# A local attention and gated feed-forward kernel on one core: orders for VectorE and GpSimd as one resource, values over 128 partitions, first mixing by TensorE, normalisation and mixing on any of three engines

## The chip, the cores and the metric

The kernel runs on one core of one Trainium2 chip. A core has TensorE (PE in the profile, with PEld for its weight loads), VectorE (DVE), ScalarE (ACT), GpSimd (POOL) and SyncE (SP), which issues all loads and stores here. The metric is device time in microseconds (us); less is better.

## The reference

Four batches, eight heads, 768 tokens, head size 64. First a local attention with pooled blocks, then a feed-forward layer with a sigmoid gate on its output:

```python
k_sum = k.reshape(B, H, nb, block, D).max(axis=3)        # block = 32, nb = 24
v_sum = v.reshape(B, H, nb, block, D).mean(axis=3)
mask_l = np.abs(pos[:, None] - pos[None, :]) < window    # window = 16
scores_l_m = np.where(mask_l, scale * q @ k.T, -1e9)
scores_s = scale * einsum(q, k_sum) + np.log(block)
a = softmax(concatenate([scores_l_m, scores_s]))
x = a @ concatenate([v, v_sum])                          # -> (4, 768, 512)

x_prev = x shifted by one token
xk = mu_k * x + (1.0 - mu_k) * x_prev
xr = mu_r * x + (1.0 - mu_r) * x_prev
k = np.maximum(xk @ w_k, 0.0)                            # 512 -> 1024
v = k * k @ w_v                                          # 1024 -> 512
r = 1.0 / (1.0 + np.exp(-(xr @ w_r)))                    # 512 -> 512
return r * v
```

The weights arrive as 64-bit numbers and are made into 32-bit ones on the chip.

## The kernel before, in words

The work falls into operations that a planner (class `Plan`, method `schedule`) puts into an order for each engine before anything is emitted; the engines then run these orders strictly. The planner is a list scheduler: every operation has a length per engine from the table `LENGTH`, a due time, and the buffers that it takes from small pools; at each step the operation that can start first goes next, and among those that are ready, the one due first. `NUDGE` shifts due times by hand, by tag: `e` for a first product, `f` for a second one (with batch, half and index), `gate`, `mix`, `set`, `unit`, and the weights `wk`, `wv`, `wr`. Where an operation has a second way (`other`), an engine takes it only if no other engine would end it earlier by the planner's reckoning. The planner's numbers decide only on the order; the times on the chip are its own.

The stages:

- **Weights** (`weight`, lines 326 to 361). Twenty pieces of 512 KB (4 of w_r, 8 of w_k, 8 of w_v), three staging buffers `st`. Each is loaded, scaled (line 323 on ScalarE or 326 on GpSimd), its sign is taken on GpSimd (line 331), two VectorE steps join the bits (lines 335, 339), a cast makes the high part (347 or 349), and a VectorE subtraction makes the low part (361). All products are made of three in a fast format: high by high, high by low, low by high.
- **Sets** (`load_set`): for each batch and pair of heads, keys and two halves of the values are loaded (line 382: tiles of 120 partitions, one for each of 120 keys of a window, by 6 windows of 128), keys are pooled on VectorE (392 to 404), values by TensorE in batch 0 (416, 436) and spread (444).
- **Units** (`unit`): for each pair and half of the tokens, scores on TensorE (480), mask and minimum on VectorE (491), exponential on ScalarE (495), the reciprocal of the sum (502), six normalisations of 128 x 120 on GpSimd (506), transposes on TensorE (513), a copy (517), the products with the values (535), and their copy to `vx` (547 or 549).
- **Mixing** (`mixes`, lines 560 to 571): a scaled copy on ScalarE or GpSimd, a multiply-add on VectorE, a cast on ScalarE to the high part, a VectorE subtraction for the low part. It is done for the gate and for the first products, for each half and pair. `mixes_pe` does the two first steps by TensorE; no half uses it before the change.
- **Gate** (612 to 628) and **experts** (644 to 702): for each half, three gates with a sigmoid; eight first products (644), relu, square, high and low part (649 to 655), and eight second products (666, the last 692), then the product with the gate and the store.

Batch 0 needs the weights, its units and its mixing at the same time. From batch 1 on, a batch's units run in between the products of the batch ahead of it. Until the first gate, up to 150 spare matmuls on the identity (line 727) keep TensorE at work where it would wait.

Of the kernel before, what the change touches and what calls it, by code (L numbers as in the profile page):

```python
# [20 lines left out]
P = 128  # L21
# [18 lines left out]
    score=900, transpose=340, vtrans=200, vpool=900, vsel=240, spread=560, spread_p=900, values=1000, values0=1750, mixe=1480, minus=200, diag=330, none=0, wminus=1250, wevac=570, gate=2790, gate_p=2100, gate32=3720, e1=2090, e1_32=2800,  # L40
    e2a=1400, e2b=700, e2=700, e2h=350, resulth=400, e2_32=2800, e2l_32=930,
    warm=220, kred=860, kred2=470, kmax=190, kcopy=340, vred=860, mask=204, rc=190, evac=475, mixd=620, sub=490, khv=340,
    result=695, wsign=720, eps=190, wor=740, wsub=625, tiny=60,
    exp=380, pts=400, vm=160, mixa=540, cast=440, relu=525, square=530, sigmoid=500, wscale=570, wcast=530,
    norm=470, wscale_p=640, wcast_p=640, mixa_p=860, kcopy_p=630, evac_a=375, fill=735,
# [9 lines left out]
WARM = 150  # L55
APART = False
MIX_PE = ()
# [4 lines left out]
    e003=-1000, e004=8000, e005=3000, e013=-40000, e016=-20000, e017=-3000, f000=-8000,  # L62
    f001=3000, f002=3000, f003=-1000, f005=1000, f006=25000, f007=9000, f010=25000,
    f011=8000, f013=3000, f014=-20000, f015=3000, f017=25000, gate01=-3000, gate10=-8000,
    mix010=-8000, set12=7000, set13=3000, unit001=-3000, unit020=1000, unit100=1000, unit101=16000,
    unit110=8000, unit111=-9000, unit120=-39000, unit130=8000, unit131=11000, wk1=3000, wk3=20000,
    wk4=3000, wk6=4000, wk7=-20000, wr0=-21000, wr3=8000, wv3=7000, wv4=3000,
    wv5=-1000, wv6=-8000, wv7=-19000,
# [7 lines left out]
BETWEEN = 5, 6, 7  # L76

# [14 lines left out]
class Plan:  # L92
# [9 lines left out]
    def op(self, eng, cost, due, emit, reads=(), writes=(), size=0, other=None):  # L102

        bufs = []
        for x, _ in list(reads) + list(writes):
            if isinstance(x, Buf) and x not in bufs:
                bufs.append(x)
        ways = {eng: (LENGTH.get(cost, 0), emit)}
        if other:
            ways[other[0]] = (LENGTH[other[1]], other[2])  # L110
        o = Op(len(self.ops), ways, due, bufs, size)
        o.tag = self.tag
        for x in reads:
# [12 lines left out]
        self.ops.append(o)
        o.name = cost
        return o

    def schedule(self):  # L130
# [20 lines left out]
        order = []  # L151

# [8 lines left out]
        spare = [o for o in self.ops if o.name == "warm"]  # L161
        while any(ready.values()):
            best = None
            for e, now in engines.items():
                pick = None
                for o, at in ready[e]:
                    start, need, ok = max(at, now, o.due - EARLY if e == "SP" else 0), {}, True
                    for x in o.bufs:
                        if x.t is None:
                            k = need.get(x.pool, 0)  # L170
                            if x.n != turn[x.pool] + k or len(free_slots[x.pool]) <= k:
                                ok = False
                                break
# [29 lines left out]
            if e == "SP":  # L203
                engines[e] = start + 60
                dma = max(dma, start + 600) + o.size * DMA_NS_PER_BYTE
                o.finish = dma + DMA_FIXED - 600
            else:
                engines[e] = start + o.cost
                o.finish = start + o.cost + TAIL[e]
            for x in o.bufs:  # L210
# [6 lines left out]
            if o.name == "gate_p" and spare:  # L217

                for w in spare:
                    for x in w.bufs:  # L220
                        x.left -= 1
                        if not x.left:
                            free_slots[x.pool].append((start, x.t))
                spare = []
                ready["PE"] = [x for x in ready["PE"] if x[0].name != "warm"]
            if o.name == "warm":
                spare.remove(o)
# [8 lines left out]
def tile_kernel(ctx: ExitStack, tc: tile.TileContext, q, k, vT, v, mask, ident, pool, sel, mu, w_k, w_v, w_r, out):  # L236
# [50 lines left out]
    for which in kinds:  # L287
        for p in range(NPAIR):
            for n, m in enumerate((om_sb, mu_sb)):
                op("POOL", "diag", None, lambda which=which, p=p, n=n, m=m: nc.gpsimd.tensor_scalar(  # L290
                    out=diag_sb[:, kinds.index(which), p, n, :], in0=ident_sb, scalar1=m[:, which, p:p + 1], scalar2=1.0,
                    op0=ALU.mult, op1=ALU.mult), reads=[*IDENT, *OM, *MU], writes=[("diag", (which, p, n))])
            op("POOL", "none", None, lambda: None, reads=[("diag", (which, p, n)) for n in range(2)], writes=[("diag", (which, p))])
# [12 lines left out]
    def weight(name, i, src, dst_h, dst_l, due=None):  # L306
# [23 lines left out]
        def sign():  # L330
            nc.gpsimd.tensor_scalar(  # L331
# [12 lines left out]
        op("POOL", "wsign", None, sign, reads=[(st, 0)], writes=[(we, 0)])  # L344
# [26 lines left out]
    def load_set(b, p):  # L371
# [9 lines left out]
        for hf in range(2):  # L381
            op("SP", "load", None, lambda hf=hf: nc.sync.dma_start(
                out=windows(vw[hf]), in_=v[b, p, hf]),
               writes=[(vw[hf], "a"), (vw[hf], "b")], size=NK * HW * 512)
# [73 lines left out]
    def unit(b, p, hf, e, due):  # L458
# [45 lines left out]
        for h in range(2):  # L504
            for i in range(NSL):
                op("POOL", "norm", None, lambda h=h, i=i: nc.gpsimd.tensor_scalar(  # L506
                    out=y[h].t[:, i, :], in0=y[h].t[:, i, :], scalar1=rc.t[:, NSL * h + i:NSL * h + i + 1],
                    scalar2=1.0, op0=ALU.mult, op1=ALU.mult),
                   reads=[(y[h], i), (rc, 0)], writes=[(y[h], i)])
# [42 lines left out]
    def mixes(b, hf, which):  # L552
# [3 lines left out]
        for p in range(NPAIR):  # L556
# [6 lines left out]
               other=("POOL", "mixa_p", lambda xt=xt, xa=xa, p=p: nc.gpsimd.tensor_scalar(  # L563
                   out=xa.t, in0=xt.t[:, lo:lo + HT], scalar1=om_sb[:, which, p:p + 1], scalar2=1.0,
                   op0=ALU.mult, op1=ALU.mult)))
# [11 lines left out]
    def mixes_pe(b, hf, which):  # L577
# [4 lines left out]
        for p in range(NPAIR):  # L582
# [3 lines left out]
            def mix(xt=xt, ps=ps, p=p):  # L586
                for n in range(2):
                    nc.tensor.matmul(
                        ps.t[:, 0:HT], diag_sb[:, kinds.index(which), p, n, :], xt.t[:, n + lo:n + lo + HT], start=(n == 0), stop=False)

            op("PE", "mixe", None, mix, reads=[*old, (xt, hf), ("diag", (which, p))], writes=[(ps, 0)])
# [133 lines left out]
    spare = pools["av"][0][:, HT:HT + P]  # L725
    for _ in range(WARM):
        op("PE", "warm", 1.0e8, lambda: nc.tensor.matmul(spare, ident_sb, ident_sb, start=True, stop=True), reads=IDENT)  # L727
# [122 lines left out]
```

## Time and profile before

| what | value |
|---|---|
| median of 3 runs | 472.68 us (472.26 to 473.19) |
| profiled execution, span | 472.4 us |
| mean granted TensorE clock | 0.989 |
| instructions | 9665 |
| moved by DMA | 51.18 MB |

The page gives no other time of the profiled execution than its span, from the first instruction to the last; the median of the runs stands 0.3 us above it. "Busy" is the time in which an engine works on an instruction, and an instruction that waits inside the engine, for memory for instance, counts as busy. A group row shows line, engine, operation, what it writes and reads, the shapes and the count, then busy time and the mean of one, then the engine's idle time before it and what ended that. The chain of waits follows the last instruction back to what released it. In the windows, each engine has its busy us and its number of instructions; then come the granted clock, the DMA share and GB/s.

### The profile page before, as it was taken

The numbers are of one execution on the slowest core, as the hardware profiler recorded it, in microseconds if no ns is written. First come the engines' busy times: TensorE is split into PE (matmuls) and PEld (weight loads), VectorE is DVE, ScalarE is ACT, GpSimd is POOL, SyncE is SP. The second block draws the span as 40 slices with busy tenths as digits, with TensorE's granted clock in tenths as the row PEclk, the third lists the DMA queues.
The fourth block names the chain that finished last, engine by engine and source line by source line (L and its number), as shares of the span: only waits on it lengthen the run. The fifth ranks groups of instructions, "written<-read, shape, count | busy, mean of one in ns | idle before, by whom it ended". The sixth has DMA issues, their size and how long they took to land.

```text
span 472.4 us, 9665 instructions
## 1 busy us (share of the span) xinstructions
PE 442.6 (94%) x3531; PEld 374.6 (79%) x3531; DVE 272.5 (58%) x825; ACT 293.4 (62%) x842; POOL 145.6 (31%) x281
## 2 busy tenths in 40 slices
PE   1698699799999999999999999999999999999996
PEld 0586486687888878997888888997888888888995
DVE  4679997999646376537355467438455455223223
ACT  2767886769788686528895756429886655232311
POOL 0469898642413131302352202303252201000000
PEclk9999989799999999999999999999999999999999
DMA  8994446777410036944100307905100010001001
GB/s 270 288 272 127 137 139 212 221 235 216 138 40 15 20 122 171 242 119 150 46 23 8 111 35 230 280 5 176 47 14 12 5 68 1 1 0 68 0 2 67
DMA packets 27159, 51.18 MB, mean 108 GB/s; under 512 B 2919, under 2 KB 15079, under 8 KB 27111
## 3 DMA queue, kind: packets, MB, share of 16 engines
q1 hardware_dynamic: 27111, 50.56, 35.8%
q8 instruction: 28, 0.46, 0.4%
q14 instruction: 20, 0.16, 0.1%
HBM read 42.49 MB, written 6.29 MB: 103 GB/s over the span
## 4 chain that ended last, share of the span: by engine, by line
PE 81%; POOL 8%; DMA 3%; ACT 2%; DVE 2%; issue 1%; SPq 1%; DVEq 0%; POOLq 0%
PE mm L644 26%; PE mm L666 24%; PE av L535 4%; PE sc L480 4%; POOL y L506 4%; PE mm L612 4%; PE mm L614 4%; PE mm L613 4%; PE pt L513 4%; PE mm L692 3%; DMA mask_sb<-in_mask 2%; DMA st<-in_w_v 1%; POOL we L331 1%; ACT y L495 1%; PE av L727 1%
## 5 line engine op out<-in xcount | busy, mean ns | idle before, releaser
L506 POOL TENSOR_SCALAR y<-y,rc 128x120 f32<-128x120 f32 x192 | 87.8, 476 | 118.6 <-DVE rc L502 114.6
L644 PE MATMUL mm<-xs,wk_h 128*128 128x384 f32 x512 | 104.3, 346 | 5.2 <-ACT r L649 3.4
L644 PEld LDWEIGHTS mm<-xs,wk_h 128*128 128x128 f32 x512 | 91.7, 192 | 9.7 <-ACT r L649 3.8
L649 ACT ACTIVATE r<-mm 128x384 f32<-128x384 f32 x64 | 31.3, 489 | 91.0 <-PE mm L644 90.6
L495 ACT ACTIVATE y<-y,mn 128x120 f32<-128x120 f32 x192 | 73.7, 387 | 5.7 <-DVE mn L491 5.5
L666 PE MATMUL mm<-wv_h,kh 128*128 128x512 f32 x168 | 68.8, 409 | 0.1
L666 PE MATMUL mm<-wv_l,kh 128*128 128x512 f32 x168 | 66.8, 398 | 0.5 <-DVE wv_l L361 0.5
L491 DVE CUSTOM_DVE_ANT_0 y<-sc,mask_sb 128x120 f32<-128x120 f32 x192 | 42.7, 275 | 24.8 <-PE sc L480 15.2
L644 PE MATMUL mm<-xs,wk_l 128*128 128x384 f32 x256 | 55.8, 340 | 0.0
L571 DVE TENSOR_TENSOR xs<-xa,xs 128x384 fp32r<-128x384 f32 x64 | 37.6, 592 | 30.0 <-ACT xs L569 29.7
L653 DVE CAST kh<-r 128x384 fp32r<-128x384 f32 x38 | 14.1, 372 | 63.5 <-ACT r L651 63.0
L666 PE MATMUL mm<-wv_h,kl 128*128 128x512 f32 x168 | 50.0, 406 | 0.0
L644 PEld LDWEIGHTS mm<-xs,wk_l 128*128 128x128 f32 x256 | 46.2, 190 | 0.0
L655 DVE TENSOR_TENSOR kl<-r,kh 128x384 fp32r<-128x384 f32 x64 | 38.1, 595 | 14.0 <-ACT kh L654 7.7
L566 DVE SCALAR_TENSOR_TENSOR xa<-vx,mu_sb,xa 128x384 f32<-128x384 f32 x64 | 42.3, 677 | 5.6 <-POOL xa L563 2.8
L563 POOL TENSOR_SCALAR xa<-vx,om_sb 128x384 f32<-128x384 f32 x23 | 18.3, 796 | 82.5 <-DVE xs L571 55.2
L480 PE MATMUL sc<-kt,qt 64*64 64x120 f32 x768 | 29.2, 280 | 14.6 <-DMA qt<-in_q 8.3
L517 ACT COPY pts<-pt 120x384 f32<-120x384 f32 x64 | 30.4, 475 | 15.6 <-PE pt L513 15.0
L612 PE MATMUL mm<-wr_h,xs 128*128 128x512 f32 x96 | 39.0, 406 | 0.0
L480 PEld LDWEIGHTS sc<-kt,qt 64*64 64x64 f32 x768 | 21.1, 138 | 22.3 <-DVE kt L404 8.3
L513 PE MATMUL pt<-ident_sb,y 128*120 128x128 f32 x192 | 34.7, 285 | 4.0 <-POOL y L506 3.7
L614 PE MATMUL mm<-wr_h,xs 128*128 128x512 f32 x96 | 38.0, 395 | 0.0
(71 smaller groups left out, 728.1 us busy)
## 6 DMA issues: line engine op xcount, KB each, us to landing
vx<-in_v SPq DMA_DIRECT2D x32, 360.0 KB
kt<-in_k SPq DMA_DIRECT2D x15, 544.0 KB
qt<-in_q SPq DMA_DIRECT2D x32, 192.0 KB
out<-z SPq DMA_DIRECT2D x23, 256.0 KB
st<-in_vT SPq DMA_DIRECT2D x12, 384.0 KB
st<-in_w_k SPq DMA_DIRECT2D x8, 512.0 KB
st<-in_w_v SPq DMA_DIRECT2D x8, 512.0 KB
st<-in_w_r SPq DMA_DIRECT2D x4, 512.0 KB
```

The costliest lines, as they stand in the source:

```text
L480: nc.tensor.matmul(sc[h].t[cs, i, 0:NK], qt.t[hs, n * QW:(n + 1) * QW], kt.t[hs, w * KB:w * KB + NK], start=True, stop=True,)
L491: op("DVE", "mask", None, lambda h=h, i=i, var=var: nc.vector.tensor_tensor_reduce(out=y[h].t[:, i, :], in0=sc[h].t[:, i, 0:NK], in1=mask_ ...
L495: op("ACT", "exp", None, lambda h=h, i=i: nc.scalar.activation(y[h].t[:, i, :], y[h].t[:, i, :], AF.Exp, bias=mn[h].t[:, i:i + 1], scale=-1.0,
L506: op("POOL", "norm", None, lambda h=h, i=i: nc.gpsimd.tensor_scalar(out=y[h].t[:, i, :], in0=y[h].t[:, i, :], scalar1=rc.t[:, NSL * h + i: ...
L513: nc.tensor.transpose(out=pt[h].t[0:NK, i * P:(i + 1) * P], in_=y[h].t[:, i, :], identity=ident_sb)
L566: op("DVE", "mixd", None, lambda xt=xt, xa=xa, p=p: nc.vector.scalar_tensor_tensor(out=xa.t, in0=xt.t[:, 1 + lo:1 + lo + HT], scalar=mu_sb ...
L571: op("DVE", "sub", None, lambda xa=xa, xh=xh, xl=xl: nc.vector.tensor_tensor(out=xl.t, in0=xa.t, in1=xh.t.bitcast(F32), op=ALU.subtract), ...
L612: nc.tensor.matmul(ps[i].t, xh.t[:, ts], wr_h[:, p, :], start=(p == 0), stop=False)
L614: nc.tensor.matmul(ps[i].t, xl.t[:, ts], wr_h[:, p, :], start=False, stop=(p == NPAIR - 1))
L644: nc.tensor.matmul(ps.t[:, 0:HT], w[:, j, p, :], x[p][s].t, start=(n == 0), stop=(n == 11))
L655: op("DVE", "sub", None, lambda: nc.vector.tensor_tensor(out=kl.t, in0=r.t, in1=kh.t.bitcast(F32), op=ALU.subtract), reads=[(r, 0), (kh, 0 ...
L666: nc.tensor.matmul(acc[t].t, a.t[:, t * P:(t + 1) * P], w[:, j, :], start=start, stop=stop)
```

## The change

- `LENGTH`, `TAIL`, `LATENCY` and the DMA rate in the planner get other numbers, mostly smaller ones, and issuing a DMA takes SyncE 430 ns instead of 60.
- The planner knows a shared port: every GpSimd operation but the smallest, and the VectorE operations in `PORT`, exclude each other in its reckoning.
- `NUDGE` is replaced by a longer table.
- Values are loaded as 128 partitions, the last 8 zeros; computation still reads 120.
- The gate's mixing of batch 0, half 0 is done by TensorE (`MIX_PE`), with the subtraction on VectorE out of PSUM; its eight diagonal matrices are made by ScalarE.
- A normalisation may run on GpSimd, VectorE or ScalarE; the first mixing step on ScalarE, GpSimd or VectorE; a weight's sign on GpSimd or VectorE.
- `mm` buffers may be taken out of turn (`LOOSE`).
- Warming matmuls run on a zeroed tile instead of the identity; as many as the planned gap holds, one for each 230 ns, stand ahead of every TensorE operation until the first gate.

The core of the diff (the old and new tables of `NUDGE` shortened):

```diff
 LENGTH = dict(
+    score=865, transpose=370, vtrans=200, vpool=900, vsel=240, spread=560, spread_p=900, values=1000, values0=1750, mixe=1480, minus=200, diag=290, wminus=1250, wevac=520, none=0, gate=2790, gate_p=2100, e1=2110,
+    e2a=1400, e2b=700, e2=700, e2h=350, resulth=340,
+    kred=860, kred2=460, kmax=90, kcopy=225, vred=865, mask=203, rc=110, evac=470, mixd=530, sub=472, psub=480, khv=300,
+    result=605, wsign=575, eps=110, wor=605, wsub=605, tiny=60, wsign_d=335,
+    exp=378, pts=362, vm=165, mixa=512, cast=405, relu=375, square=413, sigmoid=494, wscale=562, wcast=510,
+    norm=340, norm_d=165, norm_a=285, mixa_d=300, wscale_p=575, wcast_p=575, mixa_p=575, kcopy_p=400, evac_a=362,
 )
-TAIL = dict(PE=0, DVE=85, ACT=95, POOL=0, SP=0)
-LATENCY = dict(PE=260, DVE=150, ACT=170, POOL=200, SP=0)
-DMA_NS_PER_BYTE = 1 / 285.0
+PORT = ("wor", "wsub", "mixd", "sub", "khv", "kcopy", "spread", "wsign_d", "norm_d", "mixa_d")
+TAIL = dict(PE=60, DVE=85, ACT=100, POOL=30, SP=0)
+LATENCY = dict(PE=230, DVE=130, ACT=150, POOL=150, SP=0)
+DMA_NS_PER_BYTE = 1 / 390.0
...
-WARM = 150
+WARM = 230
-MIX_PE = ()
+MIX_PE = ((0, 0, 1),)
...
-    e003=-1000, e004=8000, e005=3000, e013=-40000, e016=-20000, e017=-3000, f000=-8000,
+    e000=-16000, e001=-1500, e002=-500, e003=2000, e004=1500, e005=1500, e006=-11000, e007=12500, e010=7500,
...
+LOOSE = ("mm",)
+NORM = "DVE", "ACT"
+MIXA = "POOL", "DVE"
...
+        def locks(o, e):
+            return e == "POOL" and o.kinds[e] not in ("tiny", "none") or e == "DVE" and o.kinds[e] in PORT
+
+        def begin(o, e, at):
+            at = max(at, engines[e])
+            return max(at, port) if locks(o, e) and holder != e else at
...
-                            if x.n != turn[x.pool] + k or len(free_slots[x.pool]) <= k:
+                            if x.pool not in LOOSE and x.n != turn[x.pool] + k or len(free_slots[x.pool]) <= k:
...
-                    if any(max(start, engines[f]) + c < start + o.ways[e][0] for f, (c, _) in o.ways.items() if f != e):
+                    ready_at, start = start, begin(o, e, start)
+                    if any(begin(o, f, ready_at) + c < start + o.ways[e][0] for f, (c, _) in o.ways.items() if f != e):
...
-                op("POOL", "diag", None, lambda which=which, p=p, n=n, m=m: nc.gpsimd.tensor_scalar(
+                op("ACT", "diag", None, lambda which=which, p=p, n=n, m=m: nc.scalar.activation(
...
-        op("POOL", "wsign", None, sign, reads=[(st, 0)], writes=[(we, 0)])
+        op("POOL", "wsign", None, sign(nc.gpsimd), reads=[(st, 0)], writes=[(we, 0)],
+           other=("DVE", "wsign_d", sign(nc.vector)))
...
-                out=windows(vw[hf]), in_=v[b, p, hf]),
-               writes=[(vw[hf], "a"), (vw[hf], "b")], size=NK * HW * 512)
+                out=vw[hf].t[:, 0:S].rearrange("p (w d) -> p w d", d=P), in_=v[b, p, hf]),
+               writes=[(vw[hf], "a"), (vw[hf], "b")], size=P * HW * 512)
...
+                op("POOL", "norm", None, norm(nc.gpsimd), reads=[(y[h], i), (rc, 0)], writes=[(y[h], i)],
+                   other=[x for x in (("DVE", "norm_d", norm(nc.vector)), ("ACT", "norm_a", norm_act)) if x[0] in NORM])
...
-            op("PE", "minus", None, lambda ps=ps, xh=xh: nc.tensor.matmul(
-                ps.t[:, 0:HT], minus_sb, xh.t, start=False, stop=True), reads=[(xh, 0), ("minus", 0), (ps, 0)], writes=[(ps, 0)])
-            op("ACT", "cast", None, lambda ps=ps, xl=xl: nc.scalar.copy(out=xl.t, in_=ps.t[:, 0:HT]),
-               reads=[(ps, 0)], writes=[(xl, 0)])
+            op("DVE", "psub", None, lambda ps=ps, xh=xh, xl=xl: nc.vector.tensor_tensor(
+                out=xl.t, in0=ps.t[:, 0:HT], in1=xh.t.bitcast(F32), op=ALU.subtract),
+               reads=[(ps, 0), (xh, 0)], writes=[(xl, 0)])
...
-    for _ in range(WARM):
-        op("PE", "warm", 1.0e8, lambda: nc.tensor.matmul(spare, ident_sb, ident_sb, start=True, stop=True), reads=IDENT)
...
+    still = const.tile([P, P], F32, name="still")
+    nc.gpsimd.memset(still, 0.0)
+    spare = pools["av"][0][:, HT:HT + P]
+    end, early = 600, True
     for o in order:
+        if o.eng == "PE" and early:
+            for _ in range(int((o.start - end) // WARM)):
+                nc.tensor.matmul(spare, still, still, start=True, stop=True)
+            end, early = o.start + o.cost, o.name != "gate_p"
         o.emit()
...
+    vn = np.concatenate([vn, np.zeros_like(vn[:, :, 0:P - NK])], axis=2)
+    vn = vn.reshape(B, NPAIR, P, 2, HW, P).transpose(0, 1, 3, 2, 4, 5)
```

More of the change, by code (lines that the diff above doesn't have):

```diff
@@ L61 @@
 NUDGE = dict(
-    e003=-1000, e004=8000, e005=3000, e013=-40000, e016=-20000, e017=-3000, f000=-8000,
[L63 to L67, printed above, removed]
@@ L76 @@
 BETWEEN = 5, 6, 7
+LOOSE = ("mm",)
+NORM = "DVE", "ACT"
+MIXA = "POOL", "DVE"
+FIRST_UNITS = [(hf, p) for hf in range(2) for p in range(NPAIR)]
 class Buf:
@@ L107, in op @@
                 bufs.append(x)
-        ways = {eng: (LENGTH.get(cost, 0), emit)}
-        if other:
-            ways[other[0]] = (LENGTH[other[1]], other[2])
+        ways, kinds = {eng: (LENGTH.get(cost, 0), emit)}, {eng: cost}
+        for e, kind, way in ([other] if isinstance(other, tuple) else other or []):
+            ways[e] = LENGTH[kind], way
+            kinds[e] = kind
         o = Op(len(self.ops), ways, due, bufs, size)
-        o.tag = self.tag
+        o.tag, o.kinds = self.tag, kinds
         for x in reads:
@@ L151, in schedule @@
         order = []
+        port, holder = 0, None
+        def locks(o, e):
[3 more added lines that the diff above has]
+            return max(at, port) if locks(o, e) and holder != e else at
         def released(o):
@@ L160, in schedule @@
                 released(o)
-        spare = [o for o in self.ops if o.name == "warm"]
         while any(ready.values()):
@@ L203, in schedule @@
             if e == "SP":
-                engines[e] = start + 60
-                dma = max(dma, start + 600) + o.size * DMA_NS_PER_BYTE
-                o.finish = dma + DMA_FIXED - 600
+                engines[e] = start + 430
+                dma = max(dma, start + 700) + o.size * DMA_NS_PER_BYTE
+                o.finish = dma + DMA_FIXED - 650
             else:
@@ L209, in schedule @@
                 o.finish = start + o.cost + TAIL[e]
+                if locks(o, e):
+                    port, holder = engines[e], e
             for x in o.bufs:
@@ L216, in schedule @@
             order.append(o)
[L217 to L227, printed above, removed]
             for s in o.succ:
@@ L289, in tile_kernel @@
             for n, m in enumerate((om_sb, mu_sb)):
-                op("POOL", "diag", None, lambda which=which, p=p, n=n, m=m: nc.gpsimd.tensor_scalar(
-                    out=diag_sb[:, kinds.index(which), p, n, :], in0=ident_sb, scalar1=m[:, which, p:p + 1], scalar2=1.0,
-                    op0=ALU.mult, op1=ALU.mult), reads=[*IDENT, *OM, *MU], writes=[("diag", (which, p, n))])
-            op("POOL", "none", None, lambda: None, reads=[("diag", (which, p, n)) for n in range(2)], writes=[("diag", (which, p))])
+                op("ACT", "diag", None, lambda which=which, p=p, n=n, m=m: nc.scalar.activation(
+                    diag_sb[:, kinds.index(which), p, n, :], ident_sb, AF.Copy, scale=m[:, which, p:p + 1]),
+                   reads=[*IDENT, *OM, *MU], writes=[("diag", (which, p, n))])
     def gate_due(b, hf):
@@ L327, in scale_pool, with sign @@
                 out=wc.t.bitcast(F32), in0=words()[0].bitcast(F32), scalar1=2.0**-112, scalar2=1.0, op0=ALU.mult, op1=ALU.mult)
-        def sign():
-            nc.gpsimd.tensor_scalar(
+        def sign(eng):
+            return lambda: eng.tensor_scalar(
                 out=we.t.bitcast(F32), in0=words()[0].bitcast(F32), scalar1=0.0, scalar2=1.0, op0=ALU.mult, op1=ALU.mult)
@@ L505, in unit, with norm, norm_act @@
             for i in range(NSL):
[L506 to L509, printed above, removed]
+                def norm(eng, h=h, i=i):
+                    return lambda: eng.tensor_scalar(
+                        out=y[h].t[:, i, :], in0=y[h].t[:, i, :], scalar1=rc.t[:, NSL * h + i:NSL * h + i + 1],
+                        scalar2=1.0, op0=ALU.mult, op1=ALU.mult)
+                def norm_act(h=h, i=i):
+                    nc.scalar.activation(y[h].t[:, i, :], y[h].t[:, i, :], AF.Copy, scale=rc.t[:, NSL * h + i:NSL * h + i + 1])
+                op("POOL", "norm", None, norm(nc.gpsimd), reads=[(y[h], i), (rc, 0)], writes=[(y[h], i)],
+                   other=[x for x in (("DVE", "norm_d", norm(nc.vector)), ("ACT", "norm_a", norm_act)) if x[0] in NORM])
             def transposes(h=h):
@@ L562, in mixes @@
                reads=[*old, *OM], writes=[(xa, 0)],
-               other=("POOL", "mixa_p", lambda xt=xt, xa=xa, p=p: nc.gpsimd.tensor_scalar(
+               other=[(e, kind, lambda xt=xt, xa=xa, p=p, eng=eng: eng.tensor_scalar(
                    out=xa.t, in0=xt.t[:, lo:lo + HT], scalar1=om_sb[:, which, p:p + 1], scalar2=1.0,
-                   op0=ALU.mult, op1=ALU.mult)))
+                   op0=ALU.mult, op1=ALU.mult))
+                      for e, kind, eng in (("POOL", "mixa_p", nc.gpsimd), ("DVE", "mixa_d", nc.vector)) if e in MIXA])
             op("DVE", "mixd", None, lambda xt=xt, xa=xa, p=p: nc.vector.scalar_tensor_tensor(
@@ L588, in mix @@
                     nc.tensor.matmul(
[L589 to L591 removed]
+                        ps.t[:, 0:HT], diag_sb[:, kinds.index(which), p, n, :], xt.t[:, n + lo:n + lo + HT], start=(n == 0), stop=(n == 1))
+            op("PE", "mixe", None, mix, reads=[*old, (xt, hf), *(("diag", (which, p, n)) for n in range(2))], writes=[(ps, 0)])
             op("ACT", "cast", None, lambda ps=ps, xh=xh: nc.scalar.copy(out=xh.t, in_=ps.t[:, 0:HT]),
                reads=[(ps, 0)], writes=[(xh, 0)])
[L594 to L597 removed]
+            op("DVE", "psub", None, lambda ps=ps, xh=xh, xl=xl: nc.vector.tensor_tensor(
+                out=xl.t, in0=ps.t[:, 0:HT], in1=xh.t.bitcast(F32), op=ALU.subtract),
+               reads=[(ps, 0), (xh, 0)], writes=[(xl, 0)])
             x.append((xh, xl))
@@ L734, in tile_kernel @@
         weight("wv", j, w_v[j * P:(j + 1) * P, :], *places("wv", j))
-    for hf in range(2):
-        for p in range(NPAIR):
-            unit(0, p, hf, sets[p], GATES[0] - 5000 - (3 - p) * FIRST if hf == 0 else GATES[0] + 5000 + SECOND * p)
+    for hf, p in FIRST_UNITS:
+        unit(0, p, hf, sets[p], GATES[0] - 5000 - (3 - p) * FIRST if hf == 0 else GATES[0] + 5000 + SECOND * p)
     tokens = {}
```

31 lines of the change are left out of this document (22 added, 9 removed).

## The prediction, made before the changed kernel was run

> **What bounds the kernel now.** I read the page first, for busy shares and the chain of waits; then the windows, to cut the span into stages; then the chain in order of time and the groups of instructions of the first stage.
>
> ```profile
> PE 442.6 (94%) x3531; PEld 374.6 (79%) x3531; DVE 272.5 (58%) x825; ACT 293.4 (62%) x842; POOL 145.6 (31%) x281
> ...
> DVE  4679997999646376537355467438455455223223
> ...
> POOL 0469898642413131302352202303252201000000
> ...
> PE 81%; POOL 8%; DMA 3%; ACT 2%; DVE 2%; issue 1%; SPq 1%; DVEq 0%; POOLq 0%
> ```
>
> The averages hide two stages. VectorE and GpSimd are full only in slices 3 to 10, about the first 110 us, and nearly all that is on the chain besides TensorE lies there. The windows show it:
>
> ```profile
> core 0: us, PE busy (x) PEld busy (x) DVE busy (x) ACT busy (x) POOL busy (x), PEclk, DMA share, GB/s
> 0.00:35.00 35.00, 21.08 (x314) 17.32 (x315) 20.77 (x74) 19.33 (x64) 13.36 (x31) 1.00 0.93 280
> 35.00:110.00 75.00, 64.66 (x513) 51.81 (x516) 70.58 (x167) 56.40 (x152) 57.51 (x75) 0.93 0.58 181
> 110.00:472.40 362.40, 356.88 (x2713) 305.48 (x2705) 181.11 (x586) 217.63 (x627) 74.73 (x177) 1.00 0.26 77
> ```
>
> Behind 110 us TensorE is busy 356.88 of 362.4 us, VectorE half, GpSimd a fifth: no edit to those two engines gains there. Ahead of 35 us the DMA engines are full (share 0.93). Between 35 and 110 us VectorE is busy 70.58 of 75 us, and GpSimd carries the chain:
>
> ```profile
> 15.41 1.47 PE sc L480 x24
> ...
> 22.04 1.34 PE av L727 x12
> ...
> 28.14 5.88 DMA st<-in_w_v
> ...
> 41.07 3.10 POOL y L506 x6
> ...
> 75.18 4.95 POOL y L506 x6
> ...
> 80.81 1.09 DVE we L335
> ...
> 87.70 4.21 PE mm L644 x12
> ...
> 99.59 2.08 PE mm L644 x12
> 101.67 0.78 PE sc L480 x24
> ```
>
> From 41 to 80 us the chain runs on GpSimd (8% of 472.4 us, 37.8 us), mostly the normalisations of line 506; then VectorE's weight steps; from 87.7 us TensorE to the end. So the end is set by when the start-up lets TensorE run without waiting.
>
> **The change part by part.** It works on the first 110 us.
>
> *Values over 128 partitions.* The first values load is issued at 4 us; the rates up to 10 us and behind it:
>
> ```profile
> 4.01 1.22 SPq L382 DMA_DIRECT2D vx<-in_v  x2
> ```
>
> ```profile
> 5.00:10.00 5.00, 1.48 (x24) 1.14 (x24) 3.78 (x9) 0.62 (x1) 0.08 (x3) 1.00 0.98 338
> 10.00:35.00 25.00, 19.61 (x290) 16.19 (x291) 16.99 (x66) 16.76 (x61) 12.43 (x24) 1.00 0.99 283
> ```
>
> At the same full share, 338 GB/s became 283. In the 25 us, 7.1 MB moved; the eight loads of batch 0 grow by 8 rows of 3 KB each, 0.2 MB together. If the rate returns to 338, 7.3 MB take 21.5 us: 3.5 us less. If the values loads were not what slowed it, 0.2 MB more cost 0.7 us. Range -0.7 to +3.5, value 3.5, since the rate fell when these loads came and the queue was full on both sides. The chain passes DMA until 34 us, so it counts.
>
> The Trainium skill (DMA: Bandwidth & Descriptors, the section on why a DMA increments its semaphore by 16) says that a load uses the largest number of engines up to 16 that divides its rows: 120 rows give 15, 128 give 16. By that alone the 3 MB of values would move a fifteenth faster, which is under 1 us here; the rows show a larger loss than the rule explains.
>
> *Normalisation on any engine.* GpSimd's price depends on what VectorE does at the time:
>
> ```profile
> L506 POOL TENSOR_SCALAR y<-y,rc 128x120 f32<-128x120 f32 x48 | 30.2, 647 | 5.7 <-DVE rc L502 5.6
> L331 POOL TENSOR_SCALAR we<-st 128x512 f32<-128x512 f32 x20 | 16.4, 822 | 13.9 <-DMA st<-in_w_r 10.5 <-DVE wc L339 2.4 <-DMA st<-in_w_k 0.9
> ```
>
> 647 ns on average in the first 110 us; six took 4.95 us at 75 us, 825 ns each, and 3.10 us at 41 us, 517 ns. VectorE pays too. Here are its groups in the first 35 us, then from 35 to 110 us, then one copy over the whole run:
>
> ```profile
> L339 DVE SCALAR_TENSOR_TENSOR wc<-wc,we 128x512 uint32<-128x512 uint32 x3 | 2.1, 689 | 0.2
> L361 DVE TENSOR_TENSOR wr_l<-wc,wr_h 128x512 fp32r<-128x512 f32 x3 | 2.1, 689 | 2.0 <-ACT wr_h L347 2.0
> L335 DVE SCALAR_TENSOR_TENSOR we<-st,we 128x512 uint32<-128x512 uint32 x3 | 2.0, 681 | 5.0 <-POOL vx L545 5.0
> ...
> L566 DVE SCALAR_TENSOR_TENSOR xa<-vx,mu_sb,xa 128x384 f32<-128x384 f32 x2 | 1.2, 619 | 0.1
> L571 DVE TENSOR_TENSOR xs<-xa,xs 128x384 fp32r<-128x384 f32 x2 | 1.2, 578 | 0.0
> ...
> L280 DVE TENSOR_SCALAR om_sb<-mu_sb 128x8 f32<-128x8 f32 x1 | 0.1, 150 | 0.0
> ```
>
> ```profile
> L335 DVE SCALAR_TENSOR_TENSOR we<-st,we 128x512 uint32<-128x512 uint32 x17 | 14.1, 830 | 2.2 <-POOL we L331 2.2
> L339 DVE SCALAR_TENSOR_TENSOR wc<-wc,we 128x512 uint32<-128x512 uint32 x17 | 13.0, 780 | 0.2
> L566 DVE SCALAR_TENSOR_TENSOR xa<-vx,mu_sb,xa 128x384 f32<-128x384 f32 x12 | 9.5, 806 | 0.7 <-POOL xa L563 0.7
> ...
> L571 DVE TENSOR_TENSOR xs<-xa,xs 128x384 fp32r<-128x384 f32 x10 | 7.4, 736 | 0.0
> L361 DVE TENSOR_TENSOR wv_l<-wc,wv_h 128x512 fp32r<-128x512 f32 x8 | 6.8, 850 | 1.1 <-POOL wv_h L349 1.1
> L361 DVE TENSOR_TENSOR wk_l<-wc,wk_h 128x512 fp32r<-128x512 f32 x8 | 6.5, 809 | 0.0
> ```
>
> ```profile
> L404 DVE COPY kt<-ks 128x288 f32<-128x288 f32 x11 | 3.6, 327 | 0.3
> ```
>
> Beyond the durations of the first 35 us lie 17 x 0.15 + 17 x 0.09 + 12 x 0.19 + 10 x 0.16 + 8 x 0.16 + 8 x 0.12 = 10.2 us of VectorE's 70.6: waiting that counts as busy. Without it 60.4 are left.
>
> The Trainium skill (SBUF — State Buffer, section "SBUF: two separate sides") calls the port pair that both engines share an exclusive lock, held for a whole instruction. The stretched rows on both engines agree.
>
> On VectorE a normalisation costs between 150 ns (8 elements) and 327 (288 elements); in proportion, 0.22 us at 120. The planner gives each to the engine where it ends first. Of the 48 of batch 0, some 36 (six of eight units) fall in this stage, at most 7.9 us if VectorE takes all; ScalarE, 56.4 of 75 us busy, can take some. With GpSimd rid of line 506 its chain goes, and VectorE is late next.
>
> *First mixing by TensorE.* Four of line 566 leave VectorE (4 x 0.62 = 2.5 us) and four mixing steps leave ScalarE or GpSimd; the subtraction stays, now out of PSUM, priced alike. TensorE gets eight fp32 matmuls of 384 columns. The nearest row is the warming matmul of 128 columns, 1.34 / 12 = 0.11 us: in proportion 0.33 each, 2.7 us in all; twice that if they ran at half the rate. They go where TensorE waits anyway (it is busy 21 of the first 35 us, much of it warming), so 0 on the path; all 2.7 to 5.4 if that cover is gone. Behind a mixing that waits for its values stand scores and transposes in TensorE's order.
>
> *Signs on VectorE, warming, the rest.* A sign on VectorE waits for its load there, and the masks and weight steps queue behind it. GpSimd waited 10.5 us for such loads (line 331), so a badly placed one can cost VectorE some us; the planner places few while loads are late: 0, up to 3 lost. Warming without the identity's load starts at once: the score at 15.41 us took 1.47 us, a later one 0.78: 0.7 gained. The fixed warming matmuls cost 0.11 us each where the run is ahead of its plan. Eight diagonals move to ScalarE, idle for 15 of its first 35 us: 0.
>
> *Sum.* VectorE's stage: 60.4 - 2.5 + 7.9 = 65.8 us; GpSimd still has signs and scalings, so I leave a third of the contention, 3.4: 69.2 against 75, 5.8 us gained. Loads 3.5, warm scores 0.7. At 87.7 us twelve matmuls took 4.21 us instead of 2.08 behind an idle stretch (clock 0.93 over the stage): 2.1 us, gone if TensorE no longer stops there. VectorE is idle 14.2 us of the first 35; earlier loads and orders that know the shared port should fill some, my estimate 3 of it (between 0 and 10). Together 15.1: span 457.3. The median of the runs stands 0.3 above the profiled span (472.68 against 472.4; the page lists no other time of that execution), so 457.6 us.
>
> **The rivals.** *VectorE simply takes GpSimd's place.* If it takes all normalisations and its waits stay, 70.6 - 2.5 + 7.9 = 76 of 75 us: the stage gains nothing and only the loads count, 472.7 - 3.5 = 469 us. The same comes out if the planner leaves most on GpSimd and the change hardly does what it says. For it: VectorE is 94% busy. Against: the stretched durations are waiting, not work. The Trainium skill (Perfetto Trace Analysis, Optimizing Scalar/DVE Operations) warns just so that moving work between these two engines may not help, as they share a port. The trace agrees about the sharing.
>
> *The start-up packs well.* If 10 of the 14.2 idle us fill, and all contention goes (3.4 more): 457.6 - 7 - 3.4 = 447 us. For it: three engines can now take the same work. Against: ScalarE is 75% busy in the middle stage, and the three staging buffers of the weights limit the loads.
>
> *A tighter order stalls TensorE later: slower.* The new planner's lengths are shorter, so it may put a product closer behind what it needs. In the steady stage the steps behind a first product are these:
>
> ```profile
> 409.16 0.87 PE L644 MATMUL mm<-xs,wk_l 128*128 128x384 f32 x4
> ...
> 410.07 0.49 ACT L649 ACTIVATE r<-mm 128x384 f32<-128x384 f32 x1 [3.17 <-PE mm L644]
> ...
> 411.15 0.36 DVE L653 CAST kh<-r 128x384 fp32r<-128x384 f32 x1 [3.19 <-ACT r L651]
> ```
>
> They end 1.5 us after the product. A cover of one score (0.78 us) in place of another product (2.08) would leave 0.7 us of waiting. There are 64 such steps; from 15.1 / 64 = 0.24 us each the gain is gone; at half of them stalled by 0.7 it would be 457.6 + 22 = 480 us. Against: the new lengths (0.375 + 0.413 + 0.3 us, and nearly 0.5 for its hops) add up to about 1.5 us, as measured.
>
> **How the numbers follow.** Forecast, 452 to 464 us: 0.60. VectorE in GpSimd's place, 465 to 471: 0.18. Packs well, 445 to 452: 0.13. Slower through stalls: 0.06. Gains and stalls that cancel within 0.2% (about 1 us, what a measurement can tell from no change): 0.03. Faster 0.91, same 0.03, slower 0.06. The range 447 to 469 holds the forecast and most of the two cases beside it.
>
> **What would show it.** Right: line 506 of the new kernel spread over engines and gone from the chain; lines 335 and 339 near 0.69 us; over 320 GB/s up to 30 us; all weights processed some 10 us earlier; TensorE without waits from about 75 us; behind that the same 98%. Wrong: VectorE on the chain from 35 to 90 us at unchanged durations (first rival), or TensorE idle behind 110 us (last).

## The result, and the profile after

The changed kernel takes 457.94 us (median of 4 runs, 457.84 to 458.39); the kernel before took 472.94 beside it (472.26 to 475.27). The ratio is 0.9679, with a 95% interval of 0.9651 to 0.9708. The profiled execution took 457.95 us, 1.85 us more than its span of 456.1. About the same distance stands in the other runs (471.85 us for a span of 470.1 of the kernel before), so the kernel before's profiled execution, span 472.4, was some 1.5 us above its median. The two profiled spans differ by 16.3 us, the medians by 15.0.

The page of the changed kernel, the same lines as before:

```profile
PE 448.0 (98%) x3599; PEld 378.2 (83%) x3599; DVE 298.5 (65%) x1016; ACT 296.2 (65%) x879; POOL 25.2 (6%) x54
...
DVE  5999999999773956647565547958552456243122
...
POOL 0332310001000000000000000100000000000000
...
PE 78%; DVE 16%; DMA 2%; issue 1%; ACT 1%; SPq 1%; DVEq 0%
```

GpSimd is all but empty and off the chain; VectorE has 16% of it. How much it has is not firm: the page of another run of the same kernel (457.50 us) follows the chain over VectorE only up to 50 us, then over ScalarE, and from 64 us over TensorE:

```profile
PE 87%; DVE 8%; ACT 4%; issue 1%; DVEq 0%; POOL 0%; POOLq 0%
```

So the three engines stand close to each other in the start-up. The stages of the first run:

```profile
0.00:35.00 35.00, 32.96 (x409) 27.17 (x410) 28.75 (x108) 24.90 (x90) 8.97 (x21) 1.00 0.84 308
35.00:110.00 75.00, 72.75 (x625) 57.88 (x625) 74.94 (x234) 68.58 (x199) 10.86 (x17) 1.00 0.63 210
110.00:456.10 346.10, 342.33 (x2568) 293.17 (x2567) 194.78 (x676) 202.69 (x592) 5.40 (x17) 1.00 0.23 74
```

Between 35 and 110 us TensorE is busy 72.75 us instead of 64.66, ScalarE 68.58 instead of 56.40, VectorE all of it, GpSimd 10.86 instead of 57.51, and the clock is 1.00 throughout. Behind 110 us nothing is lost that was not lost before (342.33 of 346.10 us). The loads, 5 to 10 and 10 to 35 us:

```profile
5.00:10.00 5.00, 5.00 (x51) 4.88 (x54) 4.15 (x10) 1.30 (x2) 0.00 (x0) 1.00 1.01 373
10.00:35.00 25.00, 23.95 (x353) 18.28 (x346) 23.90 (x97) 21.64 (x86) 8.56 (x16) 1.00 0.85 314
```

373 GB/s while the queue is full, and from 10 us on more bytes than before in a smaller share of the time (314 against 283 GB/s, 0.85 against 0.99). The chain of the first 110 us, in order of time:

```profile
3.52 5.75 DMA qt<-in_q
...
13.79 0.54 DVE we L355
...
34.18 2.05 DVE y L528 x5
...
58.58 1.10 DVE we L351 x2
...
94.64 0.87 DVE vs L449
95.56 0.28 PE pt L452
95.84 2.31 PE mm L671 x12
```

Before, it ran mostly on GpSimd from 41 to 80 us; now it runs on loads for 13 us and then on VectorE, step behind step, until 95. VectorE's groups between 35 and 110 us (lines 355 and 359 were 335 and 339; 594 was 566; 528 is the normalisation, 351 the sign):

```profile
L355 DVE SCALAR_TENSOR_TENSOR we<-st,we 128x512 uint32<-128x512 uint32 x15 | 10.1, 680 | 0.0
L359 DVE SCALAR_TENSOR_TENSOR wc<-wc,we 128x512 uint32<-128x512 uint32 x15 | 10.0, 676 | 0.0
...
L528 DVE TENSOR_SCALAR y<-y,rc 128x120 f32<-128x120 f32 x27 | 7.6, 336 | 0.0
L594 DVE SCALAR_TENSOR_TENSOR xa<-vx,mu_sb,xa 128x384 f32<-128x384 f32 x11 | 6.6, 608 | 0.0
...
L351 DVE TENSOR_SCALAR we<-st 128x512 f32<-128x512 f32 x12 | 5.6, 486 | 0.0
```

830 ns became 680, 806 became 608: with GpSimd all but empty these steps no longer stretch. All this looks as forecast. Whether the parts are worth what the forecast gave them, only runs can tell.

### The profile page after: what moved, and what is told of

Read it like the earlier page. It is cut to its first block, busy times and chain, and to the rows that moved or that the text cites. A ratio compares the mean times of both kernels' runs of the same rounds, so it can differ in the third digit from the quotient of the medians.

```text
span 456.1 us, 9735 instructions
## 1 busy us (share of the span) xinstructions
PE 448.0 (98%) x3599; PEld 378.2 (83%) x3599; DVE 298.5 (65%) x1016; ACT 296.2 (65%) x879; POOL 25.2 (6%) x54
## 4 chain that ended last, share of the span: by engine, by line
PE 78%; DVE 16%; DMA 2%; issue 1%; ACT 1%; SPq 1%; DVEq 0%
PE mm L671 27%; PE mm L693 24%; PE av L562 4%; PE mm L639 4%; PE mm L641 4%; PE mm L640 4%; PE pt L540 4%; PE sc L501 4%; PE mm L719 4%; DVE y L528 2%; DVE we L355 2%; DVE wc L359 2%; DVE y L512 2%; DMA qt<-in_q 1%; DVE we L351 1%
## 5 line engine op out<-in xcount | busy, mean ns | idle before, releaser
L671 PE MATMUL mm<-xs,wk_h 128*128 128x384 f32 x512 | 101.6, 340 | 0.0
L682 DVE TENSOR_TENSOR kl<-r,kh 128x384 fp32r<-128x384 f32 x64 | 35.2, 553 | 28.5 <-PE mm L693 27.6
L680 DVE CAST kh<-r 128x384 fp32r<-128x384 f32 x49 | 17.3, 358 | 55.3 <-ACT r L678 27.4
L599 DVE TENSOR_TENSOR xs<-xa,xs 128x384 fp32r<-128x384 f32 x60 | 32.5, 548 | 18.7 <-ACT xs L597 18.6
L640 PE MATMUL mm<-wr_l,xs 128*128 128x512 f32 x96 | 37.9, 395 | 0.0
L693 PEld LDWEIGHTS mm<-wv_h,kh 128*128 128x128 f32 x168 | 31.6, 188 | 7.0 <-issue 0.8
L693 PEld LDWEIGHTS mm<-wv_l,kh 128*128 128x128 f32 x168 | 31.7, 188 | 5.9
L516 ACT ACTIVATION_READ_ACCUMULATOR y<-y,mn 128x1 f32 x192 | 36.3, 189 | 0.0
L594 DVE SCALAR_TENSOR_TENSOR xa<-vx,mu_sb,xa 128x384 f32<-128x384 f32 x60 | 35.8, 611 | 0.5 <-ACT xa L587 0.2
L540 PE MATMUL pt<-ident_sb,y 128*120 128x128 f32 x192 | 32.7, 278 | 1.5 <-ACT pts L544 1.2
```

The costliest lines, as they stand in the source:

```text
L516: op("ACT", "exp", None, lambda h=h, i=i: nc.scalar.activation(y[h].t[:, i, :], y[h].t[:, i, :], AF.Exp, bias=mn[h].t[:, i:i + 1], scale=-1.0,
L540: nc.tensor.transpose(out=pt[h].t[0:NK, i * P:(i + 1) * P], in_=y[h].t[:, i, :], identity=ident_sb)
L594: op("DVE", "mixd", None, lambda xt=xt, xa=xa, p=p: nc.vector.scalar_tensor_tensor(out=xa.t, in0=xt.t[:, 1 + lo:1 + lo + HT], scalar=mu_sb ...
L599: op("DVE", "sub", None, lambda xa=xa, xh=xh, xl=xl: nc.vector.tensor_tensor(out=xl.t, in0=xa.t, in1=xh.t.bitcast(F32), op=ALU.subtract), ...
L640: nc.tensor.matmul(ps[i].t, xh.t[:, ts], wr_l[:, p, :], start=False, stop=False)
L671: nc.tensor.matmul(ps.t[:, 0:HT], w[:, j, p, :], x[p][s].t, start=(n == 0), stop=(n == 11))
```

## The experiments

Theory: the gain is faster loads, normalisations off GpSimd with the contention gone, and VectorE filled earlier. First rival: VectorE bounds the stage anyway and where a normalisation runs is worth nothing. Second rival: the new order gains by itself. All experiments but the one on the table keep the order on every engine that the planner made, and change only what is issued at a place. Each ratio is to the kernel before on the same chip; differences in us are between medians.

### Values on 120 partitions again

```diff
-                out=vw[hf].t[:, 0:S].rearrange("p (w d) -> p w d", d=P), in_=v[b, p, hf]),
+                out=windows(vw[hf]), in_=v[b, p, hf]),
```

> The changed kernel with its order on every engine kept, but values loaded as 120 partitions again. If the slow loads of the kernel before came from the 120 partitions and the start-up still hangs on them (the forecast's term of 3.5 us): the rate between 10 and 35 us falls from 314 GB/s towards 283 and the time rises by about 3.5 us, to 461.4. If only the engines' number counts (15 of 16), under 1 us: 458.5. If the loads are hidden now behind VectorE, which fills its time from 14 us on: 458, the rate lower all the same.

463.01 us, ratio 0.9799 (0.9778 to 0.9821): 5.1 us lost. Its windows from 5 to 10 and 10 to 35 us, and two waits of its TensorE:

```profile
5.00:10.00 5.00, 5.00 (x39) 4.88 (x42) 4.07 (x10) 1.31 (x2) 0.00 (x0) 1.00 0.99 322
10.00:35.00 25.00, 21.04 (x292) 15.38 (x293) 18.59 (x76) 17.29 (x67) 6.92 (x12) 0.93 0.94 287
```

```profile
24.18 2.93 PE L616 MATMUL mm<-vx,diag_sb 128*128 128x384 f32 x4 [2.19 <-ACT vx L576]
...
29.77 0.85 PE L437 MATMUL mm<-vx,pool_sb 120*32 120x128 f32 x20 [0.50 <-DMA vx<-in_v]
```

The first mixing in the changed kernel:

```profile
20.65 1.56 PE L616 MATMUL mm<-vx,diag_sb 128*128 128x384 f32 x4 [0.27 <-ACT vx L576]
```

287 GB/s again at a share of 0.94; VectorE works 18.59 of these 25 us instead of 23.90. TensorE waits, its granted clock is 0.93, and its first mixing comes 3.5 us later and takes 2.93 us instead of 1.56. The 120 partitions did slow the loads, and the start-up hangs on them. The Trainium skill (DMA: Bandwidth & Descriptors, why a DMA increments its semaphore by 16) has such loads on 15 engines instead of 16. A sixteenth does not explain it: in the same two windows the rate fell from 373 to 322 GB/s, and from 314 at a share of 0.85 to 287 at 0.94, for each busy engine by 17%. The traces keep every packet: among those of the first 35 us, a row of a values load (3072 bytes) took 121 ns at the median in the changed kernel and in the next experiment, which has 128 partitions too, but 185 ns in the kernel before and 192 in this run; a row of 4096 bytes of the weights took 159 ns in all four. So the rows of these loads themselves are slower; why, stays open.

### Values on 128 partitions in the order before

The reverse edit, in the kernel before.

> The kernel before, its order kept, with only the values loaded as 128 partitions. If the faster loads are worth the same by themselves as in the changed kernel (5.1 us between 463.01 and 457.94): 467. If they are hidden there, since the chain runs on GpSimd from 41 us on and GpSimd's work does not shrink: 471 to 473, with the higher rate in the trace and GpSimd merely starting earlier and waiting more. Forecast's term: 3.5 us, 469.

471.07 us, ratio 0.9967 (0.9952 to 0.9982): 1.6 us gained. Its first two stages:

```profile
0.00:35.00 35.00, 24.04 (x331) 19.65 (x332) 25.16 (x89) 22.39 (x79) 17.37 (x36) 1.00 0.79 293
35.00:110.00 75.00, 67.02 (x544) 54.00 (x543) 70.73 (x169) 57.74 (x158) 55.37 (x74) 0.91 0.58 190
```

The loads are earlier and VectorE does 25.16 us of work by 35 us instead of 20.77, but from there GpSimd (55.37 us) and VectorE (70.73) are as full as before, and TensorE's clock is 0.91 (0.93 before). The same loads are worth 5 us only beside the new order and its forms.

### Normalisations back on GpSimd, in the new order

```diff
-                   other=[x for x in (("DVE", "norm_d", norm(nc.vector)), ("ACT", "norm_a", norm_act)) if x[0] in NORM])
+                   other=[x for x in (("DVE", "norm_d", norm(nc.gpsimd)), ("ACT", "norm_a", norm_act)) if x[0] in NORM])
```

> The changed kernel with its order kept, but every normalisation that the planner gave to VectorE issued on GpSimd at the same place in the order. Theory: the two engines exclude each other, so a normalisation on GpSimd costs 0.5 to 0.8 us instead of 0.2 to 0.3 and VectorE's own steps stretch from 0.68 to about 0.8 us; GpSimd comes back on the chain and the middle stage loses the 5.8 us of the forecast and more, as the order was not made for it: 464 to 470. Rival: VectorE is the bound now (74.9 of 75 us busy), so taking some 13 us of work off it is a gain even at GpSimd's price: 446 to 454.

456.07 us, ratio 0.9651 (0.9625 to 0.9677): the theory's 464 to 470 is refuted. It was run again beside the changed kernel, on one chip:

> The changed kernel once more, on the same chip as the next one: 458 us.

> The changed kernel with VectorE's normalisations issued on GpSimd in the same order, once more beside the changed kernel. If the 456.07 us measured first is more than chance: 1 to 2.5 us below the changed kernel on this chip. If it was chance: within 1 us of it.

458.02 us, ratio 0.9701 (0.9682 to 0.9719), against 455.35, ratio 0.9645 (0.9625 to 0.9666). So it is 2.7 us faster than the changed kernel, and the fastest of all complete ones here. From its first run, the chain, the middle stage, GpSimd's normalisations in the first 110 us, and VectorE's groups between 35 and 110:

```profile
PE 92%; DMA 3%; DVE 2%; ACT 1%; SPq 1%; issue 0%; POOL 0%; DVEq 0%
```

```profile
35.00:110.00 75.00, 74.28 (x643) 60.98 (x642) 74.56 (x223) 71.44 (x208) 32.28 (x51) 1.00 0.65 219
```

```profile
L528 POOL TENSOR_SCALAR y<-y,rc 128x120 f32<-128x120 f32 x52 | 27.6, 549 | 23.9 <-DVE rc L523 23.9
```

```profile
L355 DVE SCALAR_TENSOR_TENSOR we<-st,we 128x512 uint32<-128x512 uint32 x15 | 10.8, 723 | 0.0
...
L359 DVE SCALAR_TENSOR_TENSOR wc<-wc,we 128x512 uint32<-128x512 uint32 x15 | 10.3, 694 | 0.0
L594 DVE SCALAR_TENSOR_TENSOR xa<-vx,mu_sb,xa 128x384 f32<-128x384 f32 x12 | 7.6, 641 | 0.0
...
L351 DVE TENSOR_SCALAR we<-st 128x512 f32<-128x512 f32 x12 | 6.4, 556 | 0.0
```

A normalisation takes GpSimd 549 ns instead of 336 on VectorE, and it stretches VectorE's steps: 15 x 43 + 15 x 18 + 12 x 33 + 12 x 70 ns, 2.2 us in these four groups, and 12 x 48 ns more in line 599. But it takes 7.6 us off VectorE in that stage. TensorE is busy 74.28 us instead of 72.75, and the chain is now nearly all TensorE's (in the second run it has 86% and VectorE 7%): there is little left that a freer VectorE could gain. The 11 normalisations of this stage that the planner gave to ScalarE stayed there.

### Normalisations on VectorE in the order before

```diff
-                op("POOL", "norm", None, lambda h=h, i=i: nc.gpsimd.tensor_scalar(
+                op("POOL", "norm", None, lambda h=h, i=i: nc.vector.tensor_scalar(
```

> The kernel before, its order kept, with only the normalisations issued on VectorE instead of GpSimd. Forecast's term: GpSimd's chain goes and the contention with it, 5.8 us gained: 467. Rival, from the run with the normalisations back on GpSimd (456.07, not slower than the changed kernel): where a normalisation runs matters little by itself, 471 to 474, since VectorE, 94% busy in that stage, takes over what GpSimd loses.

477.99 us, ratio 1.012 (1.0098 to 1.0142): 5.3 us slower, where the forecast's term said 5.8 faster. Its chain, its middle stage, and VectorE's groups there:

```profile
PE 73%; DVE 15%; DMA 6%; ACT 2%; issue 1%; POOL 1%; SPq 1%; DVEq 0%
```

```profile
35.00:110.00 75.00, 62.50 (x490) 49.96 (x488) 73.17 (x187) 54.87 (x145) 34.45 (x41) 0.93 0.55 178
```

```profile
L335 DVE SCALAR_TENSOR_TENSOR we<-st,we 128x512 uint32<-128x512 uint32 x17 | 13.1, 772 | 0.5 <-POOL we L331 0.5
...
L506 DVE TENSOR_SCALAR y<-y,rc 128x120 f32<-128x120 f32 x30 | 9.0, 314 | 0.0
L566 DVE SCALAR_TENSOR_TENSOR xa<-vx,mu_sb,xa 128x384 f32<-128x384 f32 x10 | 8.3, 829 | 0.0
```

GpSimd lost 23 us of work and its chain, which has passed to VectorE (15%, GpSimd 1%). Yet line 566 is no shorter (829 ns, 806 before) and line 335 only a little (772, 830 before): with the normalisations gone, the signs, scalings and casts that are still on GpSimd go on stretching them, and VectorE got 9.0 us more. The normalisations stand in VectorE's order at places made for GpSimd; how much of the 5.3 us is due to that was not tried. In the new order they stand where the planner put them for VectorE, and cost there too.

### Normalisations and signs on GpSimd, in the new order

The edit above, and the same for a sign that the planner gave to VectorE.

> The changed kernel, its order kept, with the normalisations and the signs of the weights that VectorE had both issued on GpSimd. If it is the signs off GpSimd that count (16.4 us of GpSimd's time in the kernel before, and VectorE's next step waits for each): GpSimd is full again between 35 and 110 us and the time goes to 462 or more. If neither counts and the gain is in the order and the loads: 455 to 459, like the run with the normalisations alone.

457.29 us, ratio 0.9683 (0.9663 to 0.9703): with both back on GpSimd the kernel is as fast as the changed one (0.9679 and, run again, 0.9701). Its middle stage, and one VectorE group there:

```profile
35.00:110.00 75.00, 73.23 (x630) 58.78 (x629) 71.30 (x202) 69.85 (x199) 41.18 (x60) 1.00 0.64 216
```

```profile
L355 DVE SCALAR_TENSOR_TENSOR we<-st,we 128x512 uint32<-128x512 uint32 x15 | 12.6, 847 | 1.4 <-POOL we L351 1.4
```

Line 355 is stretched as in the kernel before (847 ns; 830) and TensorE is as busy as in the changed kernel (73.23 us). Contention may cost something: with the signs on GpSimd too the kernel is 1.2 to 1.9 us slower than with the normalisations alone, with intervals that overlap a little. But the work that VectorE no longer has makes up for it: the contention is back and the time is that of the changed kernel.

### First mixing by ScalarE and VectorE, in the new order

```diff
-                for n in range(2):
-                    nc.tensor.matmul(
-                        ps.t[:, 0:HT], diag_sb[:, kinds.index(which), p, n, :], xt.t[:, n + lo:n + lo + HT], start=(n == 0), stop=(n == 1))
+                nc.scalar.activation(xm, xt.t[:, lo:lo + HT], AF.Copy, scale=om_sb[:, which, p:p + 1])
+                nc.vector.scalar_tensor_tensor(
+                    out=xm, in0=xt.t[:, 1 + lo:1 + lo + HT], scalar=mu_sb[:, which, p:p + 1], in1=xm,
+                    op0=ALU.mult, op1=ALU.add)
```

> The changed kernel with its order kept, but the first mixing of batch 0, half 0 is done by ScalarE and VectorE at the places where TensorE did it, and the diagonals are not made. Theory: VectorE bounds the stage, so four multiply-adds of 0.61 us cost about 2.4 us and TensorE's saving counts for nothing there: 460.3. Rival: TensorE's own work counts in the end, as it hardly waits behind 20 us; then its fp32 matmuls (6.1 us busy in the trace) come off: 453 to 456. Between them: no change, 458.

462.12 us, ratio 0.9784 (0.9755 to 0.9813): 4.2 us lost, more than VectorE's 2.4. Its first stages:

```profile
0.00:35.00 35.00, 31.52 (x361) 26.37 (x363) 25.98 (x102) 20.25 (x73) 8.35 (x19) 0.90 0.83 295
35.00:110.00 75.00, 70.24 (x617) 55.84 (x612) 74.50 (x226) 67.80 (x194) 11.46 (x18) 0.95 0.60 202
```

VectorE has done 2.8 us less work by 35 us, and the clock, 1.00 in the changed kernel, is 0.90 and 0.95. That the lower clock is what costs the rest was not tried. Taking 6.1 us of fp32 matmuls off TensorE gained nothing.

### No warming

The loop of warming matmuls is left out of the changed kernel.

> The changed kernel without its warming matmuls. Forecast's term: the first scores run cold, 1.47 instead of 0.78 us, 0.7 to 1.4 us on the path: 459. If what runs cold is hidden behind VectorE and the loads: 458. If TensorE falls back to a lower clock later, in waits that the warming now fills (clock 1.00 over all stages): 460 and more, with a granted clock under 0.99 in the first 60 us.

459.15 us, ratio 0.9712 (0.9684 to 0.9741): 1.2 us lost, with intervals that overlap, so it is not settled. The clock stayed at 1.00.

### Signs left out

```diff
-                out=we.t, in0=words()[1], scalar=29, in1=we.t, op0=ALU.logical_shift_right, op1=ALU.bitwise_or)
+                out=we.t, in0=words()[1], scalar=29, in1=zero_sb, op0=ALU.logical_shift_right, op1=ALU.bitwise_or)
```

> The changed kernel, its order kept, with the twenty sign steps left out (the weights lose their signs; the step behind reads a zero tile instead, at the same cost). It takes 7.8 us from VectorE and 2.0 from GpSimd in the first 110 us. If VectorE, busy 74.9 of 75 us, bounds the start-up: 4 to 7 us faster, 451 to 454. If TensorE's own work and the first 20 us do: 456 to 458.

This kernel computes with weights that have lost their signs. 454.96 us, ratio 0.9633 (0.9615 to 0.965): 3.0 us for 7.8 us of VectorE's work and 2.0 of GpSimd's, between the two cases that were expected. VectorE's work counts in the start-up, but each us taken off it is worth less than half a us at the end: TensorE and ScalarE are close behind it.

### The order alone

The order of the changed kernel with values on 120 partitions, the first mixing on ScalarE and VectorE, and VectorE's normalisations and signs issued on GpSimd (the edits above together). What the planner gave to ScalarE stays there, and so do the new warming and the first mixing steps on VectorE.

> The order of the changed kernel with the forms of the kernel before: values loaded as 120 partitions, the first mixing by ScalarE and VectorE, VectorE's normalisations and signs issued on GpSimd. If the prices found one at a time add up: 457.3 (normalisations and signs on GpSimd) + 5.1 (values) + 4.2 (mixing) = 467 us, and the new order by itself is worth some 5 to 6 of the 15 us. If the order's worth hangs on the forms it was made for: 472 or more. If the prices overlap, as two delays of the same 40 us: 462 to 465, and the order is worth most.

466.59 us, ratio 0.9892 (0.9871 to 0.9912), as the sum of single prices said. Its middle stage:

```profile
35.00:110.00 75.00, 69.88 (x587) 55.00 (x590) 67.63 (x190) 68.19 (x198) 40.96 (x60) 0.95 0.60 191
```

So 5.3 us stay without these forms. Against the kernel before, GpSimd works 40.96 us instead of 57.51, VectorE 67.63 instead of 70.58, and ScalarE 68.19 instead of 56.40: work has moved from the two engines that stretch each other's steps to the one that does not take part. Among it are 11 normalisations, 3.9 us of ScalarE's time in this stage, which the order before could not place there. What they are worth alone was not tried, nor what the new lengths, the shared port in the planner, the freer `mm` buffers and the new warming are worth each.

### The table of due times emptied

> The changed kernel with an empty table NUDGE, so with the due times of the planner alone; lengths, shared port, forms and loads as changed. If the planner's better knowledge makes the order: 458 to 462. If the table does, which names some 190 operations: 465 or more, most of the gain gone.

462.14 us, ratio 0.9789 (0.9771 to 0.9807). The table is worth 4.1 us (458.02 with it on this chip); the rest of the gain stands without it.

## Why the prediction was right, and where its steps were not

The time (457.6 against 457.94 us), the stage and the direction were right. The sum came out through terms that were wrong in both directions.

*Loads, 3.5 us.* Right in mechanism and place, too small: 5.1 us in the new order, 1.6 in the old one. The forecast did not see that this price depends on the order around it.

*Normalisation, "5.8 us gained".* This step failed for the move to VectorE. It took the stretching of VectorE's steps, and GpSimd's chain, for a cost of the normalisations. Put on VectorE alone they cost 5.3 us; put back on GpSimd in the new order they gain 2.7. In the old order VectorE, 94% busy, was the bound behind GpSimd's chain: with GpSimd's chain gone, VectorE has it. The working was off as well. It set 69.2 us of work against the 75 us of the stage, not against the 70.6 that VectorE worked, so 4.4 of the 5.8 us were idle time of VectorE counted as gained. A normalisation on VectorE took 0.28 us of its time (7.6 us for 27), not 0.22; and of the contention nothing was left, not a third. The forecast's own first rival said that VectorE would take GpSimd's place, and the page of the changed kernel shows half of its sign: VectorE is on the chain from 13.8 to 95 us, but its durations are not unchanged. Its time, 469 us, did not come, since the new order took work off both engines: 5.3 us that the sum did not name, but for part of its 3 us of "earlier loads and orders". That 5.3 and 5.8 nearly agree in size is chance. What the normalisations on ScalarE gained is part of these 5.3 us and was not measured by itself. The Trainium skill (Perfetto Trace Analysis, Optimizing Scalar/DVE Operations) warned that moving work between these engines might not help; the runs bear it out for the move to VectorE in the old order (5.3 us lost), not for the move back in the new one (2.7 us gained).

*First mixing, 2.5 us off VectorE and "0 on the path".* Right in direction, too small: it is worth 4.2 us. Its price on TensorE was misread as well. Here are the warming matmuls and the mixing in the changed kernel:

```profile
L788 PE MATMUL av<-still 128*128 128x128 f32 x104 | 15.9, 316 | 1.0 <-POOL still L782 1.0
...
L616 PE MATMUL mm<-vx,diag_sb 128*128 128x384 f32 x16 | 6.1, 504 | 0.3 <-ACT vx L576 0.3
```

The code issues eight mixing matmuls and the trace has sixteen records: each of these fp32 matmuls leaves two. So the 1.34 us of twelve records that the forecast scaled from were six matmuls, and a mixing matmul costs 6.1 / 8 = 0.76 us, over twice the 0.33; four mixings take 6.1 us of TensorE, a little more than the upper end given (5.4). It is paid in TensorE's waits, as the forecast had it. But it frees VectorE where it is late, and without it the clock falls. ScalarE is not freed: it makes eight diagonals, 3.2 us, in place of four scaled copies of 0.61 us.

*Warm scores, 0.7 us.* 1.2 measured, not settled. *The cold stretch, 2.1 us.* The clock is 1.00 in every stage, and twelve such matmuls take 2.31 us at 95.84 us; the stretch is gone. *VectorE's idle time.* 6.25 us are left of 14.2 in the first 35: 8 us filled, where the forecast counted 3; of these, 4.9 us are 17 normalisations that came to VectorE.

*The slower rival.* TensorE loses no more behind 110 us than before; the tighter lengths do no harm there. *The case that packs well.* It did not come: VectorE is busy 74.94 of 75 us in the middle stage, and TensorE 72.75.

*The runs' time against the span.* The forecast added 0.3 us to its span; the distance is 1.8, and the profiled execution of the kernel before was a slower one. It worked against the 1.2 us by which the span fell further than forecast (456.1 against 457.3).

## What to carry to other kernels

A chain that runs along one engine does not say that its work should go to its neighbour: look at how full the engine is that would take it, and look for one that has room and whose steps do not stretch (ScalarE here, 56 of 75 us; what it gained alone was not measured). Price a faster load, or a freed engine, with the order around it, since the same edit was worth 5.1 us in one order and 1.6 in the other. In an experiment that keeps the order and changes one engine at a time, a part that gains nothing shows at once, here even one that cost 2.7 us.

## What the runs showed of the hardware

- 120 partitions instead of 128 in the values loads lowered the rate from 373 GB/s to 322 between 5 and 10 us, and from 314 (share 0.85) to 287 (share 0.94) behind it. A row of 3072 bytes took 192 ns at the median instead of 121. That is more than a lost sixteenth; the cause is open.
- The Trainium skill (SBUF — State Buffer, "SBUF: two separate sides") calls the port pair that VectorE and GpSimd share an exclusive lock, held for a whole instruction. Steps do stretch (line 355: 680 ns with GpSimd nearly empty, 723 with normalisations on it, 847 with signs too), but 35 normalisations on GpSimd between 35 and 110 us, 20.1 us of its time, cost VectorE's lines 355, 359, 594, 351 and 599 only 2.7 us together. How much of a GpSimd instruction holds the port was not tried.
- An fp32 matmul here leaves two records in the trace (16 for 8 mixing matmuls, 768 for 384 of the scores), a transpose (192 for 192) or a product in the fast format (512 for 512 in line 671) one. Counting records as matmuls halves the price.
